# Tail keys of an attention kernel by one row group at a time, their sums in a block of 32-column tiles

## The chip, the core and the metric

The kernel runs on one core of a Trainium2 chip. A core has a matrix engine (TensorE, PE in the profile) whose 128x128 array can be split into tiles that work side by side, and VectorE (DVE), ScalarE (ACT), GpSimd (POOL) and SyncE (SP), which here only issues transfers. Engines run their own instruction streams in order and wait for each other through semaphores. TensorE reads SBUF and writes PSUM; the other engines move results from PSUM to SBUF. The metric is the device time of one launch in microseconds; lower is better.

## The reference

```
q, k, v: (8, 12, 448, 64) float32      w_in: (768, 2048)   w_out: (2048, 768)
q_n = q / (norm(q) + 1e-6)             k_n = k / (norm(k) + 1e-6)
attn = softmax(q_n @ k_n.T / 0.1)      # per batch and head, 448 x 448
x = (attn @ v), heads side by side     # (3584, 768)
h = x @ w_in;  g = h * cos(h)          # (3584, 2048)
out = g @ w_out                        # (3584, 768) float32
```

Scores are cosines over 0.1, so the kernel takes the exponential without a maximum first, and divides by the sum of exponentials afterwards.

## The kernel before

**Groups, units, batches.** Two heads form a group (48 groups; `a` is 0 or 1 for the head), three groups a unit (16 units), two units a batch (8 batches). A head has 448 tokens in seven blocks of 64: token `7 p + s` lies on partition `p` of block `s`. Keys of blocks 0 and 4, 1 and 5, 2 and 6 are paired on 128 partitions, so three blocks of 128 keys are left, and one block of 64, the tail.

**The steps of a group on TensorE.** `scores(g, c)` (line 710) computes transposed scores, keys by queries. For c = 1, 2, 3 it issues four matmuls of 64 contraction rows by 64 output columns over 448 queries, one on each quarter of the array: row group by head, column group by half of the keys. For c = 0 it takes the 64 tail keys; the queries are split into two halves `o` of 224, so that the tail fills 128 partitions too. ScalarE writes the exponentials to `PX`.

`attend(g, direct, stages)` (line 740) forms the product with v and the sums of the exponentials, in one pair of PSUM banks, `ka` for the product and `ks` for the sums. Stages 0 and 1 are the tail's (`rest`, line 751): four matmuls of 64 rows by 64 columns over 224 queries, two for the product on row group `o = n` and two for the sums (ones as weights) on the other row group. Each half of the queries sits on its own row group, so a stage writes half of the queries for the product and the other half for the sums. Stage 1 waits until stage 0 has been written (`P.settled`). Stage 2 is the block of 32-column tiles: `av` (line 765) with three rounds of four matmuls, then `sm` (line 772) and `sm2` (line 780), where four 32-column tiles form sums: for head `a`, tile 0 of its two sums block 1 of the keys, tile 1 block 2, and block 3 is shared by columns, 224 each. Partitions 64a and 64a+32 then hold two parts of each sum. For some groups stage 2 goes first (`turned`).

14 of the 48 groups are `direct`: their sums are formed for all 64 partitions and turned into reciprocals on ScalarE. The other 34 copy product and sums to `xu`, and `chain(u)` (line 885) does a unit's sums at once: two small transfers gather the two parts into `sums`, VectorE adds and inverts them (for unit 2 GpSimd), one transfer writes them to DRAM, two spread them over partitions into `RB`, and GpSimd multiplies (line 911) into `xT`, the input of the feed-forward part.

**Feed-forward.** `m1` (line 926) is the first product of a batch, 16 columns of 128 with six 128-row matmuls over 448 tokens (line 919); its first twelve matmuls read only the batch's first unit. ScalarE takes the cosine, VectorE multiplies into `gT`. The second product (`m2_quarters`, line 999) is cut into steps of four 64x64 matmuls over 384 columns, one on each quarter: for column half `x`, for row group `z`. A row group writes the bank `z ^ h`; after 16 steps `h` changes and the row groups swap banks, and that step waits for the end of the former (`P.settled`, line 1023). These steps are spread between the attention's steps as filling.

**Order.** From group 6 on TensorE's order is fixed: by `pair` and, from group 19, by a script of letters (s scores, f steps of the second product, a, b, c the stages 0, 1, 2 of `attend`, m the first product). `Program.arrange` plays the program with costs given by hand and sorts the work of the other engines and SyncE's transfers by due times, so a changed cost can move work on these engines. A change of tiling (quarters Q, 32-column C32, whole F) costs TensorE time. At the start TensorE runs matmuls on zeros (`P.filler`) until there is work.

## Time and profile before

| | |
|---|---|
| median of 3 runs | 421.23 us (420.74 to 421.92) |
| profiled execution | 420.54 us, of which the span 418.8 us |
| TensorE busy | 409.6 us, 98% of the span, mean granted clock 0.999 |
| ScalarE, GpSimd, VectorE busy | 65%, 58%, 45% |
| tail stages of all groups (line 761) | 384 matmuls on quarters, 224 columns |
| sums of the 34 groups (lines 776, 784) | 136 of 448 and 136 of 224 columns |
| second product on quarters (line 1017) | 2816 matmuls, 384 columns |

A matmul's duration in the profile includes the way through the array; the next one starts before it ends, and four on different tiles run side by side. What a matmul costs the engine is seen from the distance between starts. "Who waited for whom" counts an engine as idle only after the modelled end of its last instruction, so short waits of TensorE show as larger distances between starts rather than as idle time. In a timeline row the columns are start, duration, engine, line, operation, output and input, tile, shape, and count.

### The profile page before, as it was taken

Reading aid. Unit: us, or ns where it says so; the run is one execution under the profiler, and the core shown is the slowest. Engines: PE = TensorE matmul, PEld = TensorE weight load, DVE = VectorE, ACT = ScalarE, POOL = GpSimd, SP = SyncE. Lnnn points to the kernel's source line nnn. Section 1 sums busy time; section 2 is a strip of 40 time slices with the busy share of each in tenths; the row PEclk is TensorE's granted clock in tenths of the full one; section 3 lists DMA queues with packets and bytes.
Section 4 is the critical chain, followed back from the end, with each engine's and each line's share of the span. In section 5 each row is a group of like instructions: output and inputs, shape, how many; then the busy total and the mean of one; then the engine's idle time right before and its main releaser. Section 6 shows DMA issues by size and latency. Waiting matters only on the chain.

```text
span 418.8 us, 13571 instructions
## 1 busy us (share of the span) xinstructions
PE 409.6 (98%) x6074; PEld 236.5 (56%) x6074; DVE 189.5 (45%) x250; ACT 271.3 (65%) x363; POOL 242.7 (58%) x193
## 2 busy tenths in 40 slices
PE   7899999999999999999999999999999999999997
PEld 3354556655556555665466555665566655565565
DVE  3564744456663277124753087213862244223421
ACT  5887578983987746877498556776498745703500
POOL 4999977989761666938864782907867320020000
PEclk9999999999999999999999999999999999999999
DMA  8999999879849997579766993949966720141023
GB/s 191 251 253 226 209 223 172 213 174 198 144 104 151 207 222 185 109 168 217 168 114 127 210 242 83 147 109 212 212 123 128 161 68 3 41 121 38 2 67 85
DMA packets 80254, 63.61 MB, mean 152 GB/s; under 512 B 44996, under 2 KB 75204, under 8 KB 80196
## 3 DMA queue, kind: packets, MB, share of 16 engines
q1 hardware_dynamic: 61988, 50.06, 55.4%
q0 software_dynamic: 18048, 12.59, 20.2%
q8 instruction: 48, 0.79, 0.8%
q10 hardware_dynamic: 160, 0.10, 0.1%
q14 instruction: 10, 0.08, 0.1%
HBM read 54.98 MB, written 11.13 MB: 158 GB/s over the span
## 4 chain that ended last, share of the span: by engine, by line
PE 92%; ACT 4%; POOL 1%; DVE 1%; DMA 1%; issue 1%; SPq 0%; ACTq 0%; POOLq 0%
PE MP L1017 27%; PE SC L919 21%; PE AV L919 11%; PE SC L720 6%; PE AV L768 4%; PE MP L1046 4%; PE SC L1046 3%; PE SC L768 2%; PE AV L761 2%; PE AV L794 2%; PE MP L919 2%; ACT PX L735 2%; PE SC L728 1%; ACT cosb L948 1%; PE MP L809 1%; PE AV L1046 1%
## 5 line engine op out<-in xcount | busy, mean ns | idle before, releaser
L735 ACT ACTIVATE PX<-SC 128x896 bf16<-128x896 f32 (+1 forms) x166 | 132.8, 828 | 26.1 <-PE SC L720 18.2
L1017 PE MATMUL MP<-W,gT 64*64 64x384 bf16 x2816 | 142.3, 324 | 0.9 <-DVE qkT L707 0.6
L1017 PEld LDWEIGHTS MP<-W,gT 64*64 64x64 bf16 x2816 | 79.2, 107 | 35.7 <-PE MP L1017 3.8
L919 PE MATMUL SC<-xT,W 128*128 128x448 bf16 x468 | 94.9, 353 | 0.0
L669 POOL TENSOR_TENSOR qks<-raw,rn 128x896 bf16<-128x896 f32 (+1 forms) x48 | 79.8, 1679 | 24.6 <-ACT rn L661 24.0
L630 POOL TENSOR_TENSOR sq<-raw 128x896 bf16<-128x896 f32 x44 | 73.6, 1692 | 9.0 <-DMA raw<-in_q_dram 7.0
L948 ACT ACTIVATE cosb<-SC,cst 128x896 f32<-128x896 f32 x39 | 39.1, 1006 | 57.0 <-PE SC L919 52.6
L911 POOL TENSOR_TENSOR xT<-xu,RB 128x448 bf16<-128x448 f32 x34 | 37.8, 1136 | 60.7 <-DMA RB<-scr 60.7
L919 PEld LDWEIGHTS SC<-xT,W 128*128 128x128 bf16 x468 | 45.5, 98 | 42.8 <-ACT xu L848 0.6
L950 DVE TENSOR_TENSOR gT<-SC,cosb 128x896 bf16<-128x896 f32 x39 | 42.4, 1089 | 40.6 <-ACT cosb L948 38.3
L919 PE MATMUL AV<-xT,W 128*128 128x448 bf16 x264 | 56.7, 353 | 0.0
L984 DVE COPY osb<-MP 128x384 f32<-128x384 f32 x50 | 25.8, 553 | 66.8 <-PE MP L1017 56.1
L637 DVE TENSOR_REDUCE n<-sq 128x14 f32<-128x896 bf16 (+2 forms) x49 | 51.2, 1058 | 6.1 <-ACT sq L628 5.3
L720 PE MATMUL SC<-qkT 64*64 64x448 bf16 x504 | 45.6, 356 | 0.6 <-ACT PX L735 0.6
L919 PEld LDWEIGHTS AV<-xT,W 128*128 128x128 bf16 x264 | 25.6, 98 | 24.2 <-ACT xu L848 0.3
L948 ACT ACTIVATE cosb<-AV,cst 128x896 f32<-128x896 f32 x22 | 22.1, 1006 | 23.6 <-PE AV L919 20.7
L950 DVE TENSOR_TENSOR gT<-AV,cosb 128x896 bf16<-128x896 f32 x22 | 23.9, 1088 | 14.3 <-ACT cosb L948 14.2
L604 POOL DMA_DIRECT2D va<-in_v_dram x32 | 21.9, 692 | 7.0 <-DMA raw<-in_q_dram 4.2
L878 POOL TENSOR_TENSOR xT<-xu,RB 128x448 bf16<-128x448 f32 x8 | 9.1, 1134 | 28.5 <-ACT RB L874 28.5
L851 DVE COPY xu<-AV 128x896 f32<-128x896 f32 x13 | 14.2, 1091 | 21.5 <-PE AV L784 14.6
L552 ACT ACT_TABLE_LOAD x17 | 21.8, 1283 | 1.0 <-PEq L1335 0.7
L720 PEld LDWEIGHTS SC<-qkT 64*64 64x64 bf16 x504 | 14.4, 106 | 14.2 <-ACT PX L735 6.1
(95 smaller groups left out, 428.0 us busy)
## 6 DMA issues: line engine op xcount, KB each, us to landing
raw<-in_k_dram SPq DMA_DIRECT2D x48, 224.0 KB, 6.5
raw<-in_q_dram SPq DMA_DIRECT2D x48, 224.0 KB, 6.7
out_dram<-osb SPq DMA_DIRECT2D x54, 192.0 KB, 3.5
va<-in_v_dram POOLq DMA_DIRECT2D x32, 192.0 KB, 7.1
RB<-scr SPq DMA_DIRECT2D x18, 336.0 KB, 4.7
W<-in_moe_w_in_dram POOLq DMA_DIRECT2D x4, 768.0 KB, 15.9
W<-in_moe_w_out_dram POOLq DMA_DIRECT2D x4, 768.0 KB, 18.6
RB<-scr SPq DMA_DIRECT2D x6, 224.0 KB, 4.0
```

The lines of the kernel that those rows point to most:

```text
L630: pool(lambda e, x=x, y=y: e.tensor_tensor(y, x, x, ALU.mult), src_, dst, 0.1 + n * 1.78e-3, label="sq%d.%d" % (u, p)).pad = LATE if u > 1 ...
L637: dve(lambda e, w=w: e.tensor_reduce(out=n2v[i][:, 2 * p : 2 * p + 2, w], in_=sqv[p][:, :, w, :], axis=mybir.AxisListType.X, op=ALU.add), ...
L669: f = lambda e, s0=s0, s1=s1: e.tensor_tensor(qksv[i][:, p, s0:s1].rearrange("p s h d -> p h s d"), rawv[i][:, h, s0:s1, :], bass.AP(rn[i] ...
L720: m = e.matmul(ph[BP * o : BP * o + BP, a, 0:S], t[r, c - 1 + (NT3 + 1) * o, 0:BP], t[r, :, BP : 2 * BP], start=True, stop=True)
L735: act(lambda e: e.activation(PHv[j] if c == 0 else PXv[j][:, c - 1], ph[:, :, 0:n], ACT.Exp, scale=1.0 / TAU), keys, [("PX", j, c)], 2 * n ...
L911: pool(lambda e, p=p: e.tensor_tensor(xTv[b % 2][:, UP * i + p, :], xuv[:, u % 3, p, :], RBv[i][:, p, :], ALU.mult), [("RB", i, p), ("xa", ...
L919: t = e.matmul(ph[:, a, 0:S], W1v[:, order[c], 128 * n : 128 * n + 128], xTv[b % 2][:, order[c], :], start=(c == 0), stop=(c == NKC - 1))
L948: act(lambda e, ph=ph, cz=cz: e.activation(cosv[cz], ph[:, :, 0:S], ACT.Sin, bias=cst.ap()[:, 0:1], scale=1.0), names(gi) + ["cst0"], [("c ...
L950: dve(lambda e, ph=ph, cz=cz, gi=gi: e.tensor_tensor(gTv[:, 2 * gi : 2 * gi + 2, S * (b % 2) : S * (b % 2) + S], ph[:, :, 0:S], cosv[cz], ...
L984: dve(lambda e: e.tensor_copy(dst, po[:, 0:n]), name, [("osb", o, hf)], n, label="osb%d" % t)
L1017: r = e.matmul(POH[b][x : x + 64, 0:HW], gTv[k, y, col + x : col + x + 64], W2v[k, y, HW * b : HW * b + HW], start=(y == 0 and h == 0), st ...
L1046: r = e.matmul(po[:, 0 : w[1] - w[0]], gTv[:, y, col : col + 128], W2v[:, y, w[0] : w[1]], start=(y == 0), stop=(y == NF - 1))
```

## The change

For the 34 groups that aren't direct, a tail stage now issues only the two matmuls of the product, on one row group (`row`): stage 0 on row group 0, stage 1 on row group 1. The tail's sums move to stage 2: `sm2` multiplies the tail's exponentials by weights `tail` that put the sums of the first half of the queries on 16 partitions and those of the second half on the next 16, both in the columns of the first half. The ones used there have 16 columns of ones and 16 of zeros, so these next 16 partitions hold nothing else. Block 3 is shared as 336 and 112 columns, since the second tiles now have 224 more. The gather reads a third part, from those partitions, 32 columns to the left, with a gap of zeros ahead of each area in `xu`.

In `scores` and in the second product, row group 1 is issued first, and both of a row group's matmuls before the other's. The tail's exponentials get tiles of their own (`PH`, three instead of two), `rcp` becomes one instead of two, the logarithms of the norms are overwritten in place, and the zeros for the first matmuls lie in an output buffer. The costs given to the planner follow: 0.096 and 0.012 for the two stages, 0.15 for `sm2`.

```diff
@@ scores
-            for o in range(2):
-                for a in range(2):
+            for a in (1, 0):
+                for o in range(2):
@@ attend
+        def row(e, o):
+            r = slice(BP * o, BP * o + BP)
+            for a in range(2):
+                m = e.matmul(AVq[64 * a : 64 * a + 64, 0, :, o, :], vav[y][r, 2 * p + a, 0 if o else VS - 1, :], PHv[g % 3][r, a, :],
+                             start=(o == 0 and not swapped), stop=(o == 1 and swapped))
             return m
@@ sm
-                    t = e.matmul(av_[o : o + 32, 1, 0:S], ones.ap()[:, 32:64], PXv[j][:, n, a, :],
-                                 start=swapped, stop=False)
+                    t = e.matmul(av_[o : o + 32, 1, 0:S], ones.ap()[:, 80:112], PXv[j][:, n, a, :],
+                                 start=True, stop=False)
@@ sm2
-            for n in range(2):
-                for a in range(2):
-                    o, w = 64 * a + 32 * n, slice(S // 2 * n, S // 2 * n + S // 2)
-                    t = e.matmul(av_[o : o + 32, 1, w], ones.ap()[:, 32:64], PXv[j][:, 2, a, w],
-                                 start=False, stop=not swapped)
+            for a in range(2):
+                e.matmul(AVq[64 * a + 32 : 64 * a + 64, 1, :, 0, :], tail.ap(), PHv[g % 3][:, a, :], start=False, stop=False)
+            for a in range(2):
+                e.matmul(av_[64 * a : 64 * a + 32, 1, 0:SH], ones.ap()[:, 80:112], PXv[j][:, 2, a, 0:SH], start=False, stop=True)
+            for a in range(2):
+                t = e.matmul(av_[64 * a + 32 : 64 * a + 64, 1, SH:S], ones.ap()[:, 80:112], PXv[j][:, 2, a, SH:S],
+                             start=False, stop=True)
@@ stages of attend
-            if n < 2:
+            if n < 2 and not direct:
+                o = P.op("PE", lambda e, n=n: row(e, n), [("va", y), ("PH", g % 3)], [ka], cost=0.012 if n else HALF,
+                         mode="Q", label="R%d" % g)
+                if n:
+                    P.settled(opened[g], o)
+                opened[g] = o
+            elif n < 2:
@@ chain
-            sums[i].ap()[:, w * r : w * r + w],
-            bass.AP(xu, (32 * r * 5 + 3 + i) * UP * S, [[64 * 5 * UP * S, 2], [w, 64], [1, w]]))
-            for r in range(2)], [("xs", i, p) for p in range(n)], [("sums", i)], "sums%d" % i, 0.7,
+            sums[i].ap()[:, w * r : w * r + w], bass.AP(xu, x, [[64 * XW, 2], [w, 64], [1, w]]))
+            for r, x in enumerate((XS[i], 32 * XW + XS[i], 48 * XW + XS[i] - HQ))], ["gap"] + [("xs", i, p) for p in range(n)], [("sums", i)], "sums%d" % i, 0.7,
...
-            dve(lambda e: e.tensor_reduce(out=r, in_=sums[i].ap()[:, 0 : 2 * w].rearrange("p (r x) -> p x r", r=2),
-                                          axis=mybir.AxisListType.X, op=ALU.add), [("sums", i)], [("rcp", i)], 2 * w,
+            dve(lambda e: e.tensor_reduce(out=r, in_=sums[i].ap()[:, 0 : 3 * w].rearrange("p (r x) -> p x r", r=3),
+                                          axis=mybir.AxisListType.X, op=ALU.add), [("sums", i)], ["rcp"], 3 * w,
@@ m2_quarters
-                for x in range(0, 128, 64):
-                    for z in range(2):
+                for z in (1, 0):
+                    for x in range(0, 128, 64):
@@ start
+    for x in XS:
+        dve(lambda e, x=x: e.memset(xu.ap()[:, x - HQ : x], 0.0), (), ["gap"], HQ)
+    dve(lambda e: e.memset(tail.ap(), 0.0), (), ["tail"], 32)
+    for n in range(2):
+        dve(lambda e, n=n: e.memset(tail.ap()[BP * n : BP * n + BP, 16 * n : 16 * n + 16], 1.0), ["tail"], ["tail"], 16)
```

74 lines of the change are left out of this document (40 added, 34 removed).

## The prediction

> **What bounds the kernel now.** I read the page first (busy time by engine), then the list of who TensorE waited for, then the timeline of TensorE around the instructions that the change touches, and last SyncE's queue and the stretch where attention hands over to the feed-forward part.
>
> ```profile
> span 418.8 us, 13571 instructions
> ...
> PE 409.6 (98%) x6074; PEld 236.5 (56%) x6074; DVE 189.5 (45%) x250; ACT 271.3 (65%) x363; POOL 242.7 (58%) x193
> ...
> L761 PE MATMUL AV<-PX,ones 64*64 64x224 bf16 x136 | 18.4, 262 | 0.0
> ```
>
> TensorE is busy for 98% of the span, the next engine for 65%. The longest wait of TensorE in its list is 1.9 us, at the start. So time is matmul time, and what a matmul costs is not its 262 ns (four run at once, pipelined) but the distance from its start to the next start. That is read here (start, duration, engine, line, what):
>
> ```profile
> 113.66 0.26 PE L761 MATMUL AV<-PX,va 64*64 64x224 bf16 x1
> ...
> 113.67 0.26 PE L761 MATMUL AV<-PX,ones 64*64 64x224 bf16 x1
> 113.76 0.46 PE L728 MATMUL SC<-qkT 64*64 64x224 bf16 x4
> 113.95 0.76 PE L1017 MATMUL MP<-W,gT 64*64 64x384 bf16 x12
> 114.46 0.44 PE L720 MATMUL SC<-qkT 64*64 64x448 bf16 x4
> 114.65 0.26 PE L761 MATMUL AV<-PX,ones 64*64 64x224 bf16 x1
> 114.71 0.26 PE L761 MATMUL AV<-PX,va 64*64 64x224 bf16 x1
> 114.74 0.26 PE L761 MATMUL AV<-PX,ones 64*64 64x224 bf16 x1
> ...
> 230.63 0.26 PE L761 MATMUL SC<-PX,va 64*64 64x224 bf16 x1
> ...
> 230.73 0.27 PE L728 MATMUL SC<-qkT 64*64 64x224 bf16 x4
> 230.88 1.01 PE L1017 MATMUL MP<-W,gT 64*64 64x384 bf16 x20
> ...
> 234.65 0.36 PE L776 MATMUL SC<-PX,ones 128*32 128x448 bf16 x4
> 234.84 0.27 PE L784 MATMUL SC<-PX,ones 128*32 128x224 bf16 x4
> 235.04 0.38 PE L720 MATMUL AV<-qkT 64*64 64x448 bf16 x4
> ```
>
> The tail stage (`rest`, line 761) is a pack of four matmuls on the four quarters of the array; the next pack starts 0.096 us later (230.63 to 230.73). The last sums (line 784) take the same 0.096 plus 0.10 for the change of tiling (234.84 to 235.04). Between 113.76 and 114.74 the quarters run apart: the wait ahead of the scores at 113.76 left one quarter ahead, and three packs later the four starts of line 761, 0.01 us apart at 113.66, still lie 0.09 us apart (114.65 to 114.74). The quarters are independent, and a lead persists.
>
> ```profile
> 174.51 1.18 SPq L889 DMA_DIRECT2D sums<-xu  x2
> 177.49 1.23 SPq L686 DMA_TRANSPOSE qkT<-qks  x1
> 178.77 0.58 SPq L905 DMA_DIRECT2D scr<-rcp  x1
> ...
> 189.93 2.22 POOL L911 TENSOR_TENSOR xT<-xu,RB 128x448 bf16<-128x448 f32 x2 [8.11 <-DMA RB<-scr]
> ...
> 192.34 0.54 PE L919 MATMUL AV<-xT,W 128*128 128x448 bf16 x2
> ```
>
> This is the tightest hand-over: unit 7's last two products on GpSimd, and the first matmul that needs one of them.
>
> **The change part by part.** All against the profiled execution, 420.54 us (span 418.8 and 1.7 around it), which lies 0.69 under the median of 421.23.
>
> *Tail rows, 34 groups.* Stages 0 and 1 go from a pack of four (0.096 us) to two matmuls on one row group: 0.192 us of whole array becomes 0.096, if the other row group works on the next pack meanwhile. The independent quarters above say it can, and the new order (row group 1 first in scores and second product) puts work for the free half next in the queue. What bounds each group's gain I read from what stands between its two stages:
> - 13 groups with second-product matmuls between and no wait: the whole 0.096, 1.25 us.
> - 10 groups with only two steps (eight matmuls) between. Their stages lie 0.42 apart (281.07 to 281.49); without the first pack that would be 0.325. Stage 1 must wait until stage 0 is finished, and where only one score pack stands between, the two lie 0.34 apart at the closest (66.23 to 66.57). So some 0.03 is lost to that wait: 0.065 each, 0.65 us.
> - 6 groups in which the second product changes its half (`settled`, line 1023) between the stages. There the wait shows already: 230.73 to 230.88 is 0.15 for a pack of 0.096. The wait runs from the last matmul of the former half, so the second product starts no earlier, the lead is used up, and stage 1 costs its 0.096 as before: nothing gained.
> - 5 groups where the scores wait for another engine by 0.08 to 0.4 us between the stages (59.88, 109.80, 113.76, 168.49), or where a single score pack lies between (106.96): nothing gained.
> Of the 13, two (163.14, 305.34) lie ahead of waits of 0.21 and 0.36 that would swallow the gain: minus 0.19. Gain 1.71 us; bounds 0 (half-array matmuls don't overlap) and 34 x 0.096 = 3.26.
>
> The Trainium skill, "TensorEngine Tiling (Array Packing)", Restrictions and Gotchas, says that different row tiles cannot access the same PSUM bank at once and that software must see to it. Rows of this case agree as far as they go: the half change, at which the two row groups swap banks, is where the kernel waits (230.73). By the rule alone these six groups could not overlap even without that wait; without wait and rule the sum would be 0.58 lower.
>
> *Block of sums, 34 groups.* Line 776 stays. Line 784 (224 columns on each of four column tiles, 0.096) becomes 224 + 112 on two tiles and 336 on the two others: 336/224 x 0.096 = 0.144, and two more starts at 3 ns, so 0.146. Plus 0.050 x 34 = 1.70 us. Six of these stand ahead of waits of 0.08 or more (at 63, 110, 114, 169, 171, 309) that hide 0.30. Net loss 1.40. Low end 1.3; high end, if the three pairs went one after another (0.096 + 0.144 + 0.048 = 0.288), 34 x 0.19 = 6.5; I take the low one, as the trace shows tiles starting 3 ns apart everywhere.
>
> *Order of row groups in scores and second product.* Line 794 already issues in row pairs and starts every 0.19 us (65.67, 65.86, 66.05), like line 720 in turn. Zero; a nanosecond per pack either way would be 0.9.
>
> *Gather of three parts, 13 chains.* SyncE issues one transfer more, 0.59 us each (1.18 for two). At unit 7 the spread stands behind a transpose until 178.77, while the reduction ended 177.57, so 0.6 is covered there. First matmul on the last unit's product against that product's end: 146.2 against 143.0, 192.33 against 191.06 (second: 193.09 against 192.16), 239.3 against 234.4, 288.4 against 286.2, 378.8 against 375.2. Cost zero while the delay stays under 0.9 us; past that, each us costs one. Behind the gather on SyncE wait transposes; they land 3.6 us after issue and are read two groups later, with some 4 us to spare. VectorE's reduction reads 63 instead of 42 values (0.18 us now), GpSimd gets one more sum of 0.21 before a wait of 1.22 us: zero. The single `rcp` makes a reduction wait for the former spread: 121.57 and 129.99 are the closest, the spread between them is issued at 122.39 and lands in 1.7. Zero.
>
> *Start.* Five more memsets on VectorE (0.06 each) stand ahead of the zeros that the warming matmuls wait for (1.90). These end 0.35 us before the first transposes can begin (8.46): zero, without that cover 0.3.
>
> *Buffers.* The tail's exponentials get a third buffer, since the sums read them later: no new wait. In-place norms wait for a scaling two units back, and a group alone takes 4.67 us (65.67 to 70.34), a unit three of them: zero.
>
> *Planner.* It places other engines anew. TensorE's order stays; on SyncE a transpose slips behind two loads or a broadcast in four places (1.3 us against 4 or more to spare), on GpSimd a load of v moves ahead of two products whose matmul has 3 us. Zero; end up to 1 us if a new wait appears.
>
> Sum: -1.71 + 1.40 = -0.31, so 420.2 profiled, 420.9 as median.
>
> **The rivals.** A measurement tells about 0.3% (1.26 us) from no change.
> - *Forecast:* gain and cost nearly cancel, 420.9; 419.9 to 422.2 with the small ends. Chance 0.51.
> - *Everything overlaps:* the waits at half changes and between close stages move along. 34 x 0.096 - 1.70 = 1.56 less: 419.7. For it: busy share of 98% and few waits. Against: waits of TensorE for itself are distances in time and don't shrink. Chance 0.21.
> - *Rows don't run side by side* (the change doesn't do what it says): each half pack still holds the array for 0.096. Gain 0, loss 1.40: 422.6, slower. It decides once fewer than two groups gain. For it: in the trace no pack leaves quarters unused. Against: 113.76 to 114.74. Chance 0.15.
> - *A late product:* the chain slips by more than the 0.9 us at 192. Unit 7's broadcast landed some 7 us after its issue (181.98 to 189.93) against a median of 4.7, so one or two us more are possible: 421.9 to 422.9, slower. Against: the gather's extra is covered. Chance 0.13.
>
> Faster by over 0.3%: 0.22 (the second case and a little of the first). Slower: 0.27 (third and fourth, less what stays within). Same: 0.51. The range 419.5 to 422.7 leaves out the ends of the second and fourth cases and the 6.5 us.
>
> **What would show it.** Tail matmuls of line 777 two by two, with the second product's first pair starting within 0.01 us of them and its second pair 0.096 later; 0.15 from the tail sums to the end of the block; at half changes a wait of 0.15 in place of 0.05; no wait at the first matmul of units 5, 7 and 11. Wrong if the pack after a stage starts whole 0.096 later (third case), if waits at half changes vanish (second), or if TensorE waits for GpSimd's product near 192 (fourth).

## The result and the profile after

The changed kernel takes 422.3 us (median; 420.29 to 427.41), the kernel before on the same chip 420.99 us (420.37 to 422.21). The ratio is 1.0031, interval 1.0017 to 1.0045: slower by about 1.3 us, where the prediction had 0.3 us gained against the median of before. A few executions ran at a lower granted clock and took longer: the highest of the changed kernel, 427.41 us, at 0.996, and three of the eleven of run e8 below, 424.84 to 425.01 us at 0.995 to 0.996, without which e8's median of 422.75 us would be 421.7. The profiled execution took 423.07 us (span 421.3) against 420.54 (418.8).

The head and the busy line of the changed kernel's page, and the engines on the chain that ended last:

```profile
span 421.3 us, 13454 instructions
...
PE 411.2 (98%) x6006; PEld 241.0 (57%) x6006; DVE 190.2 (45%) x255; ACT 271.5 (64%) x363; POOL 243.1 (58%) x194
...
PE 78%; SPq 6%; DMA 6%; ACT 4%; POOL 2%; DVE 1%; issue 1%; POOLq 0%; ACTq 0%; DVEq 0%
```

TensorE has 68 matmuls fewer and is still busy for 98%, but the chain now runs through SyncE's queue and its transfers for 12% of the span (1% before). So the place to look is what TensorE waits for. Its waits from 34 us on (releaser, total, times, longest):

```profile
PE SC L729 <- ACT PX L744: 0.7, 2, 0.4
PE MP L1041 <- DVE qkT L716: 0.6, 1, 0.6
PE MP L943 <- POOL xT L902: 0.6, 1, 0.6
PE MP L1041 <- issue: 0.5, 1, 0.5
PE AV L943 <- DVE gT L974: 0.4, 1, 0.4
```

Before, this list had the 0.6 for `qkT` and 0.4 for `PX` and nothing of the third to fifth line. These three are new: a product of GpSimd at 91 us, a stop "for issue" at 314 us, and a gate product of VectorE at 161 us.

The parts that the prediction costed on the array look as it said. TensorE's timeline, a tail stage and the block of sums:

```profile
228.57 0.37 PE L792 MATMUL SC<-PX,ones 128*32 128x448 bf16 x4
228.76 0.31 PE L800 MATMUL SC<-PX,ones 128*32 128x336 bf16 x1
...
228.86 0.22 PE L802 MATMUL SC<-PX,ones 128*32 128x112 bf16 x2
229.01 0.38 PE L729 MATMUL AV<-qkT 64*64 64x448 bf16 x4
...
232.31 0.26 PE L777 MATMUL SC<-PH,va 64*64 64x224 bf16 x2
232.33 0.33 PE L737 MATMUL SC<-qkT 64*64 64x224 bf16 x4
232.57 1.01 PE L1041 MATMUL MP<-W,gT 64*64 64x384 bf16 x20
```

The scores start 0.02 us after a half pack (before 0.096 after a whole one), and from the last sums to the scores it is 0.25 (228.76 to 229.01; before 0.20). At this half change nothing is gained, as the prediction has it: from the tail stage to the second product it is 0.26 (232.31 to 232.57; before 0.25, 230.63 to 230.88).

Where the time went is easiest to see between the starts of the first product, which runs once per batch. Each column is the stretch that ends where that product starts in the kernel before; the numbers are microseconds more than before in one profiled execution (label as below).

```
                     to 34   to 86  to 144  to 190  to 237  to 286  to 333  to 377  end    total
after                +0.25   +0.04   +0.56   +0.85    0.00   -0.10   +0.94   -0.05  +0.02   +2.52
e1_two_gathers       +0.13   +0.14   -0.17   +0.03   +0.04   -0.10   -0.06   -0.05  +0.01   -0.04
e2_before_third      +0.01    0.00   -0.18   +0.02   +0.01   -0.01   +1.22   -0.01   0.00   +1.06
e3_zeros_first       -0.09   +0.04   -0.17   +2.28    0.00   -0.11   +0.64   -0.05   0.00   +2.55
e5_old_order         +0.05   +0.04   -0.13   +1.46   -0.02   -0.10   +0.41   -0.06   0.00   +1.65
e6_reduce_later      +0.12   +0.04   -0.17   +0.03    0.00   -0.10   +1.21   -0.05   0.00   +1.08
e7_third_on_act      +0.14   +0.04   -0.17   +0.03    0.00   -0.10   +0.19   -0.05   0.00   +0.07
e8_no_third_2_6      +0.50   +0.04   -0.17   +1.93    0.00   -0.10   +0.19   -0.05   0.00   +2.34
e9_code_shift        +0.13   +0.04   +0.36   +0.03    0.00   +0.50   +0.76   -0.05   0.00   +1.76
e10_load_order       +0.03   +0.04   -0.13   +0.03   +0.01   -0.11   +0.42   -0.05   0.00   +0.25
e12_before_reordered -0.04    0.00   +0.54    0.00    0.00   -0.01   +0.65    0.00  +0.01   +1.16
e13_early_reduce     -0.04   +0.04   -0.17   +0.03    0.00   -0.10   +0.67   -0.05  +0.01   +0.39
```

From 34 us on, where no stop falls into a stretch, the changed kernel and its variants agree to 0.04 us (e1 once to 0.1): +0.04, -0.17, +0.03, 0.00, -0.10, -0.06 (e1) or +0.19 (e7 and e8, where TensorE waits 0.2 us longer for `PX` at 309 us), -0.05. That sums to -0.31 with the one and -0.06 with the other; the prediction's sum was -0.31. The loss lies in a few stretches on top of it. In the changed kernel's profile these are three of about the same size, the stretches to 144 us (0.73 above -0.17), to 190 us (0.82 above +0.03) and to 333 us (0.75 to 1.00 above the others), and the start.

How the one to 190 us looks in the changed kernel. SyncE's queue, VectorE around 160 us, and TensorE:

```profile
145.94 1.45 SPq L1012 DMA_DIRECT2D out_dram<-osb  x2
147.49 8.17 SPq L913 DMA_DIRECT2D sums<-xu  x3
155.70 2.51 SPq L600 DMA_DIRECT2D raw<-in_k_dram  x1
```

```profile
155.18 1.08 DVE L974 TENSOR_TENSOR gT<-SC,cosb 128x896 bf16<-128x896 f32 x1
159.62 0.23 DVE L925 TENSOR_REDUCE rcp<-sums 128x21 f32<-128x63 f32 x1 [3.36 <-DMA sums<-xu]
159.88 0.29 DVE L928 RECIPROCAL rcp<-rcp 128x21 f32<-128x21 f32 x1
160.08 1.03 DVE L974 TENSOR_TENSOR gT<-AV,cosb 128x896 bf16<-128x896 f32 x1
```

```profile
161.26 2.43 PE L943 MATMUL AV<-xT,W 128*128 128x448 bf16 x12 [0.42 <-DVE gT L974]
```

And SyncE and VectorE in the kernel before:

```profile
145.77 1.64 SPq L889 DMA_DIRECT2D sums<-xu  x2
147.45 3.60 SPq L590 DMA_DIRECT2D raw<-in_k_dram  x1
...
156.30 0.19 DVE L901 TENSOR_REDUCE rcp<-sums 128x21 f32<-128x42 f32 x1
```

Unit 6's three gathers occupy SyncE's queue for 8.17 us (two took 1.64 before, at 145.77, and the load behind them 3.60), the third issue alone 5.77. VectorE stands in its reduce until the sums land at 159.62. The gate product behind it is not late by its own input, but by its place in the queue; the first product needs the bank that it frees, and TensorE waits at 161.26. Before, the reduce stood one place further back, behind a reduce of squares, and ran at 156.30 without a wait.

The product of GpSimd at 91 us, GpSimd's queue and TensorE in the changed kernel:

```profile
86.09 1.13 POOL L935 TENSOR_TENSOR xT<-xu,RB 128x448 bf16<-128x448 f32 x1 [1.76 <-DMA RB<-scr]
87.17 2.67 POOL L614 DMA_DIRECT2D va<-in_v_dram  x4
89.83 1.17 POOL L902 TENSOR_TENSOR xT<-xu,RB 128x448 bf16<-128x448 f32 x1
```

```profile
91.06 0.55 PE L943 MATMUL MP<-xT,W 128*128 128x448 bf16 x2 [0.56 <-POOL xT L902]
```

The planner has put four issues of value loads ahead of this product, where the kernel before has two, and unit 2's broadcast, issued at 81.56, is late besides. The other versions with four issues there (e10's broadcast is issued at 78.86, its product ends at 89.64 instead of 91.00) do not wait. So this 0.6 us belongs to one profile.

### The profile page after: what moved, and what is told of

It is laid out like the page before. It is cut to its first block, busy times and chain, and to the rows that moved or that the text cites. A ratio compares the mean times of both kernels' runs of the same rounds, so it can differ in the third digit from the quotient of the medians.

```text
span 421.3 us, 13454 instructions
## 1 busy us (share of the span) xinstructions
PE 411.2 (98%) x6006; PEld 241.0 (57%) x6006; DVE 190.2 (45%) x255; ACT 271.5 (64%) x363; POOL 243.1 (58%) x194
## 4 chain that ended last, share of the span: by engine, by line
PE 78%; SPq 6%; DMA 6%; ACT 4%; POOL 2%; DVE 1%; issue 1%; POOLq 0%; ACTq 0%; DVEq 0%
PE MP L1041 21%; PE SC L943 18%; PE AV L943 10%; PE SC L729 5%; PE AV L784 4%; PE MP L1070 4%; DMA sums<-xu 4%; PE SC L1070 3%; PE MP L1100 2%; ACT PX L744 2%; SPq L695 2%; PE SC L784 2%; SPq L913 2%; PE MP L943 1%; SPq L1012 1%
## 5 line engine op out<-in xcount | busy, mean ns | idle before, releaser
L744 ACT ACTIVATE PX<-SC 128x896 bf16<-128x896 f32 x126 | 113.0, 918 | 20.8 <-PE SC L729 18.6
L1041 PEld LDWEIGHTS MP<-W,gT 64*64 64x64 bf16 x2816 | 83.9, 107 | 35.3 <-issue 4.1
L640 POOL TENSOR_TENSOR sq<-raw 128x896 bf16<-128x896 f32 x44 | 73.6, 1691 | 11.8 <-DMA raw<-in_q_dram 8.7
L744 ACT ACTIVATE PH<-SC 128x448 bf16<-128x448 f32 x40 | 21.9, 546 | 6.4 <-PE SC L737 6.0
```

The source lines that it names most:

```text
L640: pool(lambda e, x=x, y=y: e.tensor_tensor(y, x, x, ALU.mult), src_, dst, 0.1 + n * 1.78e-3, label="sq%d.%d" % (u, p)).pad = LATE if u > 1 ...
L744: act(lambda e: e.activation(PHv[g % 3] if c == 0 else PXv[j][:, c - 1], ph[:, :, 0:n], ACT.Exp, scale=1.0 / TAU), keys, [("PX", j, c) if ...
L1041: r = e.matmul(POH[b][x : x + 64, 0:HW], gTv[k, y, col + x : col + x + 64], W2v[k, y, HW * b : HW * b + HW], start=(y == 0 and h == 0), st ...
```

## The experiments

Ratios are to the kernel before, measured on the same chip beside each run (its medians 421.07, 421.04, 421.02 and 420.95 us). Theory at the start: the third transfer, which the prediction had costed at nothing. Rivals: the array's gain is missing, or the start.

**e1, no third transfer.**

```diff
-            for r, x in enumerate((XS[i], 32 * XW + XS[i], 48 * XW + XS[i] - HQ))]
+            for r, x in enumerate((XS[i], 32 * XW + XS[i]))]
```

> The changed kernel with two gather transfers instead of three (the tail's sums of the second half of the queries are left out of the divisor, so the output is not the reference's). Theory 'gather': the third transfer, queued on SyncE among loads, delays the sums and, behind them, VectorE's and GpSimd's other work, and costs some 1.6 us; without it the kernel stands 0.3 us under the kernel before (ratio 0.999, at most 1.000). Theory 'array': the half packs and the longer block of sums cost the 1.3 us on TensorE; then the ratio stays at 1.003.

Measured 420.63 us, ratio 0.9992 (0.9983 to 1.0001): the loss is gone. Taken alone this says "the transfer". It says less than that: with a cheaper gather the planner also left two pieces of work on GpSimd and VectorE where they were before, which I saw only later.

**e2, the third transfer in the kernel before.** It reads a third part that nobody uses; the reduce waits for it all the same.

```diff
-            sums[i].ap()[:, w * r : w * r + w],
-            bass.AP(xu, (32 * r * 5 + 3 + i) * UP * S, ...
-            for r in range(2)]
+            sums[i].ap()[:, w * int(r + 0.5) : w * int(r + 0.5) + w],
+            bass.AP(xu, (int(32 * r) * 5 + 3 + i) * UP * S, ...
+            for r in (0, 1, 1.5)]
```

> The kernel before with a third gather transfer of the same size that nobody reads (and the zeros for the first matmuls in an output buffer, to make room). Theory 'gather': slower by 1.3 to 1.6 us, ratio 1.003 to 1.004. Theory 'array': ratio 1.000.

Measured 420.96 us, ratio 0.9997 (0.9985 to 1.001). Thirteen transfers more cost nothing there, though SyncE is held up as well (5.69 us for the three, 8.17 in the changed kernel):

```profile
146.47 5.69 SPq L889 DMA_DIRECT2D sums<-xu  x3
152.20 0.67 SPq L590 DMA_DIRECT2D raw<-in_k_dram  x1
```

So the theory falls in its simple form. Something else of the change must go with it.

**e3, the zeros of the start first.**

```diff
-    zero = dve(lambda e: e.memset(zt, 0.0), (), ["zt"], S)
+    zero = dve(lambda e: e.memset(zt, 0.0), (), ["zt"], S, bias=-2000.0)
```

> The changed kernel with the memset of the zeros put first on VectorE, so that the warming matmuls begin about 0.9 us instead of 2.2 us into the span. Theory 'start': the later zeros cost 0.3 us by the first stages (first product at 34.18 instead of 33.92), so 0.3 or more comes back: ratio 1.002 or less. Theory 'gather' alone: unchanged, 1.003.

Measured 422.92 us, ratio 1.0035 (1.0023 to 1.0046). The first product starts 0.09 us earlier than before, not 0.25 later, and nothing of it arrives at the end. The start is not it. The same wait for `gT` as in the changed kernel is 2.1 us long here (stretch to 190: +2.28).

**e4, the order of the row groups alone, in the kernel before.**

```diff
@@ scores
-            for o in range(2):
-                for a in range(2):
+            for a in (1, 0):
+                for o in range(2):
@@ m2_quarters
-                for x in range(0, 128, 64):
-                    for z in range(2):
+                for z in (1, 0):
+                    for x in range(0, 128, 64):
```

> The kernel before with only the order of row groups changed in scores and second product. My step: zero, ratio 1.000 (within 0.001). If issuing a row group's two matmuls in succession costs a nanosecond per pack, 0.9 us and 1.002.

Measured 421.0 us, ratio 0.9999 (0.9989 to 1.0009): zero.

**e5, the old order in the changed kernel** (e4's diff the other way round).

> The changed kernel with the row groups issued in the order of before, in the scores and in the second product: no two matmuls on one row group follow each other free of it, so that the new tail rows can no longer run beside the steps. Theory 'the array came out as costed' (the rows' overlap is worth the 1.71 us of the sum, and the loss is elsewhere): 1.7 us slower than the changed kernel, ratio to before 1.007 (1.005 to 1.009). Rival 'the overlap is worth little, and the loss is the rows': as the changed kernel, ratio 1.003. In the trace: second matmul of a tail row no longer at 0.01 us behind the first, and the M2 pair behind it at 0.096 us and not 0.003.

Measured 422.05 us, ratio 1.0034 (1.0018 to 1.005), as the changed kernel. Both theories had something wrong. The overlap is there without the new order; in e5's timeline matmuls of the second product on the free row group start between the two of a tail stage:

```profile
229.24 0.26 PE L777 MATMUL SC<-PH,va 64*64 64x224 bf16 x1
229.24 0.32 PE L1041 MATMUL MP<-W,gT 64*64 64x384 bf16 x1
229.24 0.26 PE L777 MATMUL SC<-PH,va 64*64 64x224 bf16 x1
229.25 0.58 PE L1041 MATMUL MP<-W,gT 64*64 64x384 bf16 x7
```

So e5 took nothing away, and the value of the overlap stayed open until e14.

**e6, unit 6's reduce later on VectorE.** Only VectorE's order changes.

```diff
-    "late": {9: 1.0, 11: 1.2, 13: 1.0},
+    "late": {6: 7.0, 9: 1.0, 11: 1.2, 13: 1.0},
```

> The changed kernel with one thing moved: VectorE's reduce of unit 6's sums and its reciprocal stand three gate products later (before the sixth one of the second block instead of before the third last of the first five); TensorE's and SyncE's orders are the same to the instruction. Theory 'the blocked gather costs through VectorE's order' (the reduce waits 3.4 us for the third part, with a gate product behind it that the first product needs): the stage from 144 to 192 us loses its extra 0.85 us of the profiled run and what other executions lose there (2.28 in the run with zeros first), so 0.8 to 2 us less than the changed kernel, ratio to before 0.999 to 1.0015. Rival 'the loss is spread over the 13 chains or is the transfers' own load': no change against the changed kernel, ratio 1.003.

Measured 422.01 us, ratio 1.0031 (1.0016 to 1.0047). In the trace the mechanism is right to the hundredth: the stretch to 190 us has its +0.03. In the time nothing is gained. The profiled execution has lost its time elsewhere, in the stretch to 333 us. TensorE there:

```profile
313.61 0.35 PE L1041 MATMUL MP<-W,gT 64*64 64x384 bf16 x2 [0.81 <-issue]
```

A wait "for issue" has no releaser in the profile. It had stood in the profiles of the changed kernel, e2 and e3 as well, at about the same place.

**e7, the third part of units 2 and 6 on ScalarE's queue.**

```diff
-        dma("SP", [lambda e, r=r, x=x: e.dma_start(
+        parts = [lambda e, r=r, x=x: e.dma_start(
...
+        dma("SP", parts[0:2] if u in (2, 6) else parts, of, to, "sums%d" % i, 0.7,
...
+        if u in (2, 6):
+            dma("ACT", parts[2:3], of, [("sums", i, 1)], "third", 0.2, "third%d" % u)
```

> The changed kernel with the third part of the sums of units 2 and 6 issued by ScalarE and the other two by SyncE as before; the other eleven chains keep three on SyncE. Theory 'a third issue is blocked in SyncE's queue until earlier transfers have gone' : on ScalarE's queue the issue takes under 1 us, the part lands with the other two, unit 6's reduce does not wait, ratio to before 0.999 to 1.002. Rival 'the sixteen engines themselves are behind, whichever queue asks': the part lands as late as in the changed kernel, ScalarE is held up too, ratio 1.003 to 1.006.

Measured 421.04 us, ratio 1.0 (0.9989 to 1.0011). The issue took 0.54 us on ScalarE for unit 6 (1.29 for unit 2), so a third issue is not slow in itself; it is slow at the end of SyncE's queue. (ScalarE issues it 3 us ahead of SyncE's two, so the time differs too.) But the reduce could start only at 159.34 all the same, and the planner had put it later, as in e6. Unit 9's value load stands ahead here too (GpSimd issues it at 141.77): a version with the load ahead that loses nothing. Neither theory was right about the landing.

**e8, no third transfer in units 2 and 6.**

```diff
+        R = 2 if u in (2, 6) else 3
-            for r, x in enumerate((XS[i], 32 * XW + XS[i], 48 * XW + XS[i] - HQ))]
+            for r, x in enumerate((XS[i], 32 * XW + XS[i], 48 * XW + XS[i] - HQ)[0:R])]
```

> The changed kernel without the third transfer in the chains of units 2 and 6 alone (it leaves their part out of the divisor; the other eleven chains keep it). Theory 'two chains carry the loss, the one before the second block's first product and the one before its gate products': as with no third transfer at all, ratio to before 0.9992 to 1.0005. Rival 'all thirteen carry it, through the load on the queues': two thirteenths of 1.65 us less than the changed kernel, ratio 1.0025. Between them, 1.001 to 1.002, would be a third place, the 0.9 us gap near 314 us that has no cause in the profile.

Measured 422.75 us (421.7 without the three named at the top), ratio 1.0039 (1.0016 to 1.0061). No theory had that. With only two parts, issued by 150.04, the sums of unit 6 land later still:

```profile
160.48 0.20 DVE L925 TENSOR_REDUCE rcp<-sums 128x21 f32<-128x42 f32 x1 [4.71 <-DMA sums<-xu]
```

So it is not the third part alone that is late. What else changed there? GpSimd's queue, in the changed kernel:

```profile
135.87 3.33 POOL L935 TENSOR_TENSOR xT<-xu,RB 128x448 bf16<-128x448 f32 x3 [3.04 <-DMA RB<-scr]
142.62 1.34 POOL L614 DMA_DIRECT2D va<-in_v_dram  x2 [3.42 <-PE AV L784]
143.96 2.26 POOL L935 TENSOR_TENSOR xT<-xu,RB 128x448 bf16<-128x448 f32 x2
146.14 1.34 POOL L614 DMA_DIRECT2D va<-in_v_dram  x2
...
150.74 1.34 POOL L614 DMA_DIRECT2D va<-in_v_dram  x2
```

and in the kernel before:

```profile
141.90 2.24 POOL L911 TENSOR_TENSOR xT<-xu,RB 128x448 bf16<-128x448 f32 x2 [3.38 <-DMA RB<-scr]
144.07 1.34 POOL L604 DMA_DIRECT2D va<-in_v_dram  x2
...
148.67 1.34 POOL L604 DMA_DIRECT2D va<-in_v_dram  x2
...
151.63 1.34 POOL L604 DMA_DIRECT2D va<-in_v_dram  x2
```

The load of unit 9's values, the last of the three before, goes first now and ahead of two products. The three issues come 1.4, 2.5 and 0.9 us earlier, while the 16 transfer engines also work on SyncE's queue. This is the move that the prediction names under its step "Planner".

**The stops "for issue".** The table of transfer queues in the changed kernel's profile has queues for code; on `q8 instruction: 47, 0.77, 0.8%` came 47 transfers of 16 KB, and 47 x 256 is 12032, nearly the number of TensorE's records (12131: matmuls, weight loads and 119 others). I numbered these records and listed, over all eighteen profiled executions of this study, each distance of 0.4 us or more from one start to the next, after 30 us, for which the trace has no releaser:

```
execution               record (modulo 256)        last start before, us    distance, us
e2_before_third         9921 (193)                 315.3                1.18
after                   9665 (193)                 314.2                0.86
e3_zeros_first          9665 (193)                 314.5                0.50
e6_reduce_later         9665 (193)                 312.5                1.13
e9_code_shift           8385 (193), 9921 (193)     270.0, 317.5         0.69, 0.41
e11_order_and_shift     1729 (193), 9921 (193)     71.2, 317.4          0.86, 0.41
e12_before_reordered    3009 (193), 9921 (193)     113.7, 316.0         0.73, 0.62
e13_early_reduce        9665 (193)                 312.3                0.58
e14_whole_packs         2241 (193)                 83.1                 0.73
e16_order_and_zeros     9665 (193)                 312.2                0.51
```

All thirteen have the same remainder, 193, so they stand at the same place of a stretch of 256 instructions; I call such a stretch a page of code and this place its first record (16 KB are 256 instructions of 64 bytes). In the ones with the changed kernel's code near 313 us the stop ends 2.3 to 2.7 us after the start of a code transfer. My reading, which only e9 tests: when TensorE enters a page, the next one is asked for, and a page lasts about 5.3 us in steps of the second product; if the transfer starts more than some 2.7 us late, TensorE runs dry. In e6 the page was asked for near 306.5 us, SyncE issued the broadcast of unit 12's reciprocals at 305.67, that broadcast moved 128 pieces of 5376 bytes from 306.95 to 311.20, and the code transfer began at 311.03. The Trainium skill, "DMA: Bandwidth & Descriptors", Queues, rings and completion order, says that a transfer engine takes turns between queues packet by packet and empties a whole packet first. The trace agrees as far as it goes: the code waited for about as long as the broadcast took.

**e9, e6 with the code shifted.** Each warming matmul at the start is cut in two: same time, 70 instructions more.

```diff
-    P.filler = (lambda e, shut: e.matmul(PO[:, 0:S], zt[:, 0:128], zt, start=shut, stop=shut), zero, MM, 0.3)
+    def warm(e, shut):
+        for x in range(2):
+            c = slice(S // 2 * x, S // 2 * x + S // 2)
+            m = e.matmul(PO[:, c], zt[:, 0:128], zt[:, c], start=shut, stop=shut)
+        return m
+    P.filler = (warm, zero, MM, 0.3)
```

> The run with unit 6's reduce later, with one thing more: each warming matmul at the start is issued as two of half the width, 70 more instructions on TensorE in the same time, so that all later work lies 70 instructions further on in TensorE's code. In four profiles TensorE stood still for 0.5 to 1.2 us near 314 us, at the one place in the code, each time until 2.3 to 2.6 us after a 16 KB transfer of code had begun; the transfer had begun 4.1 to 4.5 us after it could have, behind the broadcast of unit 12's reciprocals. Theory 'TensorE waits for its code': the request goes out 1.2 us earlier, ahead of the broadcast, and the stop near 313 us is gone or under 0.3 us; 1.0 us less than with the reduce later alone, ratio to before 0.999 to 1.0015. Rival 'the third transfer holds up something else there': the stop stays at the same matmul, ratio 1.003.

Measured 421.75 us, ratio 1.0015 (1.0002 to 1.0027). The stop left its matmul, as the theory of the code says, but it did not vanish: there are two others now, at the starts of other pages, which lie 70 instructions earlier in the work. That the stops follow the pages and not the work is shown; that a shift gets rid of them was wrong.

**e10, unit 9's value load behind unit 8's.**

```diff
-    "queue": (("bcast13", "out18"), ... ("gather6", "load u9 p0"), ...
+    "queue": (("bcast13", "out18"), ... ("load v u8", "load v u9"), ("gather6", "load u9 p0"), ...
```

> The changed kernel with one wish to the planner: unit 9's value load behind unit 8's on GpSimd, as in the kernel before. By that alone the planner puts VectorE's reduce of unit 6 back behind the next reduce of squares as well; TensorE's and SyncE's orders stay the same to the instruction, with three gathers each. Theory 'the planner's two moves, not the third transfer, delay the second block': the third part lands by 157.5 us, VectorE waits under 0.5 us for it, and the stage from 144 to 192 us is as long as before (within 0.15 us); the stop near 314 us stays, so the ratio to before is 1.0015 to 1.0035, as with the reduce later. Rival 'the third issue alone holds the gather up': it lands near 159.5 us again, the stage is 0.8 to 2.3 us longer, ratio 1.003 to 1.005.

Measured 420.8 us, ratio 0.9992 (0.9979 to 1.0005). One load in its old place takes back the loss, with all thirteen third transfers still there: better than either theory had it. (By it the planner also puts VectorE's reduce back and swaps some work on ScalarE near 170 us; SyncE's order stays.) SyncE's queue for unit 6 and VectorE's reduce:

```profile
146.80 6.19 SPq L913 DMA_DIRECT2D sums<-xu  x3
153.03 0.67 SPq L600 DMA_DIRECT2D raw<-in_k_dram  x1
```

```profile
157.30 0.23 DVE L925 TENSOR_REDUCE rcp<-sums 128x21 f32<-128x63 f32 x1 [0.96 <-DMA sums<-xu]
157.44 1.08 DVE L974 TENSOR_TENSOR gT<-AV,cosb 128x896 bf16<-128x896 f32 x1
```

VectorE has the sums 2.3 us earlier than in the changed kernel (157.30 against 159.62; 0.9 of that is there before, as the first product starts at 143.86 against 144.77), and the gate product behind the reduce is in time. The wait of 0.96 is above the 0.5 expected.

**e11, e10 with the code shifted** (both diffs).

> The changed kernel with both: the value loads in the order of before, and the warming matmuls in halves. Theory 'order of the loads plus wait for code' (the two together are the whole loss): ratio to before 0.9985 to 1.0005, near the 0.9992 without any third transfer. Rival 'the third transfer costs on its own, 13 times': ratio 1.002 to 1.003.

Measured 421.56 us, ratio 1.001 (0.9996 to 1.0024). The shift made e10 worse: its profile has a stop of 0.86 us at 71 us and one of 0.41 at 317. A shift seems to be worth some tenths in both directions (e9 against e6 0.3 less) and cannot be steered like this.

**e12, the kernel before with the changed kernel's two moves.** Two gathers, nothing else of the change.

```diff
-    "queue": (("bcast13", "out18"), ... ("gather6", "load u9 p0"), ...
+    "queue": (("bcast13", "out18"), ... ("load v u9", "x15"), ("g2.3", "sum6"), ("sum6", "red8.2"), ("gather6", "load u9 p0"), ...
```

> The kernel before, two gathers a chain, with the planner's two moves of the changed kernel and nothing else of the change: unit 9's value load on GpSimd ahead of the last two products of unit 5, and VectorE's reduce of unit 6 one place earlier; TensorE and SyncE as before to the instruction. Theory 'the planner's two moves delay the second block': the gather lands near 158 to 160 us, the stage from 144 to 192 us is 0.8 to 2.3 us longer, ratio to before 1.002 to 1.005. Rival 'only with the third transfer': ratio 1.000 (0.999 to 1.001).

Measured 421.3 us, ratio 1.0002 (0.9989 to 1.0015). By the time the rival was right: with two gathers the reduce has the sums at 156.79 in spite of the load, waits 0.89 us, and the stretch to 190 us is as before. But the copy is not exact. The third of the three value loads is issued here at 152.91, in the changed kernel at 150.74:

```profile
142.31 1.34 POOL L604 DMA_DIRECT2D va<-in_v_dram  x2 [3.84 <-PE AV L768]
...
152.91 1.34 POOL L604 DMA_DIRECT2D va<-in_v_dram  x2
```

**e13, e10 with the reduce held at the early place.**

```diff
+    ("load v u8", "load v u9"), ("g2.3", "sum6"), ("sum6", "red8.2"),
```

> The changed kernel with the value loads in the order of before, and unit 6's reduce held on VectorE at the early place that the changed kernel gives it, so that only the load's place differs there. Theory 'the load delays the gather, the reduce passes the delay on, and either alone costs little': the third part lands near 157.3 us instead of 159.6 to 160.2; the gate product behind the reduce comes 0.5 to 1 us later than with the load order alone, and the stage from 144 to 192 us is at most 0.4 us longer; ratio to before 0.999 to 1.001. Rival 'the reduce's place is the cause': the stage is 0.8 to 2.3 us longer, ratio 1.002 to 1.005.

Measured 420.81 us, ratio 0.9998 (0.9989 to 1.0006), stretch to 190 us +0.03. The reduce waits 1.73 us in its early place (a reduce of squares now stands between it and the gate product) and costs nothing, since the sums are there at 156.97. The ratios of all versions that leave the array's work alone (e16 follows below):

| | load in its old place | load ahead |
|---|---|---|
| two gathers | 1 (before); 0.9992 (e1); 0.9999 (e4) | 1.0002 (e12) |
| three gathers | 0.9997 (e2); 0.9992 (e10); 0.9998 (e13); 1.0008 (e16); 1.001 (e11, shifted) | 1.0031 (after); 1.0035 (e3); 1.0034 (e5); 1.0031 (e6); 1.0015 (e9, shifted) |
| units 2 and 6 with the third part on ScalarE, or without it | | 1.0 (e7); 1.0039 (e8) |

With three gathers on SyncE the versions with the load ahead are the slower ones without exception, whatever the place of the reduce; the two nearest, e9 and e11, overlap in their intervals. That the load needs the third transfers to do harm is not shown: e12 speaks for it, but with its own order of loads, and e8, with two parts in unit 6, loses 1.93 us in the stretch to 190 us.

The traces also have each transferred piece. The time from the first issue of unit 6's gather to the end of its last piece of 84 bytes, in us:

| | load in its old place | load ahead |
|---|---|---|
| two parts | 6.1 (before); 6.6 (e1); 9.0 (e4) | 11.2 (e8); 8.0 (e12) |
| three parts | 9.1 (e2); 9.6 (e10); 8.8 (e11); 8.7 (e13); 11.8 (e14); 8.7 (e15); 8.7 (e16) | 11.8 (after); 12.4 (e3); 12.0 (e5); 11.5 (e6); 11.6 (e7, third on ScalarE); 10.9 (e9) |

With the load ahead the gather takes longer, except in e12; but e14 shows that it can be as late with the load in its old place.

**e14, half packs filled up again**, on top of e10. The added matmuls do not leave the sums as they should be, so its output is not the reference's; only the time is read.

```diff
             for a in range(2):
+                z = slice(BP - BP * o, 2 * BP - BP * o)
+                e.matmul(av_[64 * a : 64 * a + 64, 1, 0 : S // 2], ones.ap()[z, 64 - 64 * o : 128 - 64 * o], PHv[g % 3][z, a, :],
+                         start=True, stop=True)
+            for a in range(2):
                 m = e.matmul(AVq[64 * a : 64 * a + 64, 0, :, o, :], ...
```

> The changed kernel with the value loads in the order of before, and each half pack of tail rows filled up to the old pack of four: two more matmuls of 224 columns on the other row group, whose sums the next block overwrites. This takes back what the half packs gain and nothing else. Theory 'the other row group's work runs beside them, as the sum had it': 1.71 us more than with the load order alone (0.8 to 2.5, as 272 more instructions also move the pages of code), 422.5 us, ratio to before 1.003 (1.001 to 1.0055). Rival 'the halves gain nothing, as the order of the row groups made no difference': no more than the load order alone, ratio 0.999 to 1.0005.

Measured 422.45 us, ratio 1.0041 (1.0028 to 1.0053). Against e13, measured beside it and equal to e10 but for the reduce's place, that is 1.6 us more by the medians and 1.8 by the ratios. Not all of this is the array's. The filled packs also wait for the bank of the sums, and e14's profile (the longest of its five executions by 1 us) has a stop of 0.73 us at a page and the late sums of unit 6 again:

```profile
160.10 0.23 DVE L929 TENSOR_REDUCE rcp<-sums 128x21 f32<-128x63 f32 x1 [2.57 <-DMA sums<-xu]
...
161.47 0.73 PE L947 MATMUL AV<-xT,W 128*128 128x448 bf16 x3 [0.35 <-DVE gT L978]
```

In the stretches without either (to 144, 237, 286 and 377 us) it is 1.11 us longer than e13's. So the half packs do gain, 1.1 us of it in these stretches, and the 1.71 of the sum fits the times.

**e15, the block of sums as small as before**, on top of e10.

```diff
-            for a in range(2):
-                e.matmul(AVq[64 * a + 32 : 64 * a + 64, 1, :, 0, :], tail.ap(), PHv[g % 3][:, a, :], start=False, stop=False)
...
-                e.matmul(av_[64 * a : 64 * a + 32, 1, 0:SH], ones.ap()[:, 80:112], PXv[j][:, 2, a, 0:SH], start=False, stop=True)
+                e.matmul(av_[64 * a : 64 * a + 32, 1, 0 : S // 2], ones.ap()[:, 80:112], PXv[j][:, 2, a, 0 : S // 2], ...
```

> The changed kernel with the value loads in the order of before, and the block of sums cut back to the size of before (four matmuls of 224 columns, none for the tail keys): it leaves the tail keys and, for half the queries, parts of the last full chunk out of the divisor. Theory 'the block costs 0.050 us in each of 34 groups': 1.4 us less than with the load order alone (0.7 to 1.9), 419.4 us, ratio to before 0.996 (0.9945 to 0.998). Rival 'the larger block costs nothing': ratio 0.999 to 1.0005.

Measured 420.18 us, ratio 0.998 (0.9971 to 0.999): against e13 0.6 us less by the medians and 0.8 by the ratios, half of what was expected. Its profile has no stop at a page and is 1.3 us shorter than e13's (span 417.8 against 419.1), but 0.7 of that is e13's stretch to 333 us with its stop.

**e16, e10 with the zeros first** (e3's diff added).

> The changed kernel with the value loads in the order of before, and the zeros for the warming matmuls written first on VectorE. Theory 'the start is worth what the first stage shows': up to 0.15 us less than with the load order alone, ratio to before 0.9985 to 0.9995, the best of the versions. Rival: no difference that can be measured from the load order alone, 0.999 to 1.0005.

Measured 421.33 us, ratio 1.0008 (0.9996 to 1.002). No gain; the first product starts 0.18 us earlier than before, and a stop of 0.51 us at a page takes it back. No version here that computes the reference's output is measurably faster than the kernel before; e10 is the changed kernel without its loss.

## Why the prediction was wrong, step by step

The forecast was 0.3 us less, measured are 1.3 more. That 422.3 still lies within the stated range, 419.5 to 422.7, is luck: its upper part stands for rows that do not overlap and for a late product at 192 us, and neither happened. The step that failed is "Planner", which was put at zero.

*What bounds the kernel:* right. TensorE is at 98% in both, and every loss that a profile shows was a wait of TensorE.

*Tail rows, -1.71:* about right in size (e14: 1.6 to 1.8 by the times, 1.1 in the stretches that nothing else disturbs). Its reason was half wrong. The quarters do run apart, but the new order of row groups, which the step counts on, is not needed (e5).

*Block of sums, +1.40:* mis-sized. Each block does cost 0.05 us more where it stands (0.25 against 0.20), but taking it back brought 0.6 to 0.8 us (e15) and not 1.40. The rest may be hidden behind later waits, more than the 0.30 that I took off; no run shows it.

*The sum, -0.31:* the stretches without a stop give -0.06 to -0.31, and e10 lies 0.2 us under before. The two measured terms, -1.6 to -1.8 and +0.6 to +0.8, would make about -1.0. Both e14 and e15 move the pages of code (by a shift alone e11 lies 0.8 us above e10), so neither term is good to better than that; the difference is not resolved.

*Order of row groups, 0:* right (e4). *Start, 0:* right in effect; the warming does end later (first product +0.25 in the changed kernel's profile), but putting the zeros first gained nothing (e3, e16). *Buffers, 0:* no wait on the shared `rcp` or the third `PH` shows in the trace; neither was tried alone.

*Gather of three parts, 0:* right for the transfer by itself (e2, e10, e13), and for another reason than given. The slack of 0.9 us at 192 us, on which the step rests, was never touched. The issue was not 0.59 us but up to 5.8 when SyncE's queue was long, and still cost nothing where the sums were there by 157.3. For unit 2 GpSimd waits 2.18 us for the sums in the changed kernel's profile (0.03 before), but 2.21 in e1 with two gathers. The product that TensorE waits for at 91 us is not among the hand-overs that the step lists.

*Planner, 0:* this is the step that failed. It says "on GpSimd a load of v moves ahead of two products whose matmul has 3 us. Zero". I priced what stands behind the load on GpSimd, the two products, and they were indeed in time. I did not price the load's own transfers: they share the 16 transfer engines with SyncE's queue, which at this moment carries unit 6's gather. With the load ahead the gather takes 11.8 us from its first issue, in e10 9.6; VectorE has the sums at 159.62 instead of 157.30, and with the reduce one place earlier the gate product behind it comes too late: 0.85 us in the changed kernel's profile, 1.46 to 2.28 in e5, e8 and e3. Undoing that one move took back 1.5 us (422.3 to 420.8, e10; the same in e13 with the reduce early). That much is shown. The path from the move to the time is shown in part only: the wait at 161 us is a third of what the changed kernel's profile loses, and how a load's transfers hold up the gather is argued, since e14's gather is as late without the move. The step's end of 1 us "if a new wait appears" was the right kind, and was not followed to the engine and the queue where it would appear. That TensorE stops for its own code stands in no step at all.

*The rivals.* "A late product" had the nearest time (421.9 to 422.9) and the right nature, a chain through the gather that slips, but the wrong place: nothing was lost at 192 us. (Its broadcast, 181.98 to 189.93, took 8.0 us to GpSimd's start and not "some 7".) "Rows don't run side by side" had the time 422.6 too, and e14 shows that it is false; a time that fits does not speak for its cause. "Everything overlaps" is refuted at the half change (0.26 against 0.25 us).

*What stays open.* e6 has the wait at 161 us removed and is no faster than the changed kernel. Its profile explains 0.7 of the 1.2 us that it lies above e10 and e13 (a stop of 1.13 us at a page against 0 to 0.58, and a start 0.1 to 0.2 later), and that profiled execution, 421.63 us, was the shortest of all of e6's. What the others lost, a single profile cannot show. e7 has the load ahead and the reduce later as well, without a stop: its profile is 1.0 us shorter than e6's, all of it in the stretch to 333 us, and its median is 1.0 less. So the stop may be what e6 loses; one profile of each does not show it.

## What to carry to other kernels

When a planner moves a load, price its transfers and not only what stands behind it on its engine: ask which queue is full at that time, what small transfer lies in it, and which engine stands in order behind that transfer's reader. An experiment that leaves work out also changes what a planner does with the rest, so compare the order on every engine before reading its time (e1 pointed at the transfer; e10 kept the transfer and lost nothing). And a kernel with 98% of its time on one engine may still be waiting for its own code: look whether unexplained stops fall on multiples of a page.

## What the runs showed of the hardware

- TensorE's code comes in 16 KB transfers (47 in the changed kernel, for 12131 records), and TensorE can run dry: thirteen stops of 0.41 to 1.18 us, all at the same place of 256 instructions. The Trainium skill, "Runtime: NRT & Kernel Launch", Instruction fetch mechanics, has blocks of 16 KiB and 256 instructions, in agreement with these counts, and calls the cost of crossing a boundary "mostly hidden". Here it was hidden at most boundaries, and 0.4 to 1.2 us at these thirteen.
- Moving the code by 70 instructions, in the same time, moved the stops to other work (e9) and cost e11 0.8 us against e10.
- A transfer issue on SyncE takes 0.6 us, but 4.4 to 5.8 us in five of the thirteen third gathers of the changed kernel's profile; if there are only two, the issue that follows is held instead (a load took 3.60 us before, 4.39 in e1). Issued by ScalarE, 3 us ahead of SyncE's two (143.66 and 146.76), it took 0.54 us (e7).
- Matmuls on the free row group start beside a half pack in either order of issue, within 0.02 us of it where nothing else holds them (232.31 and 232.33 in the changed kernel, 229.24 in e5).
